# A lag of two steps and a larger share of expert work in an attention and expert kernel

## The chip, the cores and the metric

The kernel runs on one core of one Trainium2 chip. The metric is the device time of one execution in microseconds (us). A core has five engines that run side by side and wait for each other through semaphores: TensorE (PE, matrix products; PEld is its loading of the stationary operand), VectorE (DVE), ScalarE (ACT), GpSimd (POOL) and SyncE (SP), which in this kernel issues nearly all transfers (DMA).

## The reference, cut to what matters

Three stages follow each other on the same 2304 rows of 512 numbers: an attention whose mask lets each block of 64 positions see its own and all earlier blocks, four experts that all rows go through, and a last pair of products with a softmax-like gate and a normalisation.

```python
# q, k, v: (4 sequences, 8 heads, 576 positions, 64)
scores = SCALE * q @ k.T
scores = where(block_i >= block_j, scores, -1e9)
attn = exp(scores - max);  attn = attn / (sum(attn) + 1e-9)
x = attn @ v                                   # to (2304, 512)
p = domain_probs / (sum(domain_probs) + 1e-9)
for e in range(4):                             # w1: 512 x 1024, w2: 1024 x 512
    h = maximum(x @ w1[e], 0)
    out += p[:, e:e + 1] * (h @ w2[e])
h = out @ w_in;  e = exp(h - max);  sm = e / (sum(e) + 1e-9)
ln = normalised(h * sm) * g_ln
return ln @ w_out
```

## The kernel before

**Tiles.** The rows are cut into 18 token tiles of 128 rows, numbered by `TILES` (line 35): tiles 0 and 1 hold the first blocks of two sequences each, and then each sequence has four tiles, i = 1 to 4, whose rows see 64 + 128 i keys (192, 320, 448, 576). The attention goes through 84 steps: two for tile 0 and two for tile 1, four (two heads each) for a tile with i of 1 to 3, eight (one head each) for one with i = 4. Counted from 0, tile 3 begins at step 8, tile 7 at 28, tile 13 at 56, tile 14 at 64, and tile 17 ends with step 83.

**A step.** It has three parts. `step_a` (line 568) is the scores: on PE the query in two parts times the keys (L600, L601) and a mask product (L604) into one of two PSUM places `sps`, then on DVE the maximum (L606 or L608) and its scaling (L610). `step_b` (line 614) is the softmax: ACT's exponential (L639, tile `p`) and its copy to fp16 (L643, `hl`), DVE's remainder (L644, `hl`), and one transposing DMA `pT<-hl` that SP issues (L651, shown as L86, since all of SP's transfers go through a helper). `step_c` (line 656) is the product with the values, `pv<-v,pT` on PE (L670), 64 columns a matmul. `hl` has two places, `pT` has two, and `pv` has one.

**Lag.** `step()` (line 834) emits the scores and the softmax of step n, and then the products of all steps up to n - LAG, with LAG = 1. A tile's last product is followed by `finish` (line 694): DVE divides by the sums (L706 to L712), the rows are scaled, split in two fp16 parts and transposed (`xT<-xh`).

**Expert work.** All matrix operands are split in two fp16 parts, so a product of the experts is three matmuls. A hidden chunk (`emit_h`, line 294) is 12 matmuls per 128 hidden columns and row group (L305, `hps`; 384 columns each for a group of three tiles), which ACT (L313) and DVE (L314) take out of PSUM as `hch`; an output (`emit_o`, line 318) is 24 matmuls of 512 columns (L325, `ops`), added up on DVE (L349). `hps` and `ops` share three PSUM places. The tokens go through the experts in two parts: part 1 is tiles 0 to 5, part 2 is tiles 6 to 17. While the attention runs, the kernel works on part 1 with all four experts and on part 2 with the first; the other experts on part 2 and the last two products come after it. The weights are loaded by SP into one place `stage` in four pieces, squared on ACT (L126) for a scale, and split on ACT (L260) and DVE (L263) into one of three places `wt`; the steps of this are spread over the expert units (line 968). Rows that have been through the last expert are transposed as `x2T<-xh` (line 392).

**What sets the order.** The loop at line 999 emits either an attention step or an expert unit. It keeps two running costs: `tdv` grows with each attention step by 1.2 times the DVE cost that `cost()` (line 848) gives, `tpe` by the PE cost of steps and expert units. An attention step comes when `tdv <= tpe + 2`, so an expert unit is emitted whenever DVE is estimated to be ahead:

```python
if not ok or tdv <= tpe + 2.0:
    at1.step()
    a, c = at1.cost()
    tdv, tpe = tdv + a * 1.2, tpe + c
```

The emitted program then goes through a scheduler that fixes each engine's order by its own estimates of time: what is emitted earlier has priority, but an instruction that it thinks not ready is passed by later ones. On the chip each engine takes its instructions in that fixed order. A place of a pool that is taken anew waits until the last reader of what lay there is done.

**Places of part 2.** The pool `xT1` holds the transposed rows of part 2 in four places, `xT0` to `xT3`, one for three tiles each. Until tile 6 and later need them they hold operands of the first tiles; `xT3` (tiles 15 to 17) holds two pieces of the first sequence's values (`vrs[1]`, line 872).

Of the kernel before, what the change touches and what calls it, by code (L numbers as in the profile page):

```python
# [9 lines left out]
F16 = mybir.dt.float16  # L10
# [10 lines left out]
NT, D, F, E = 2304, 512, 1024, 4  # L21
# [5 lines left out]
PBITS = 14  # L27
# [4 lines left out]
LAG = 1  # L32

# Token tiles: the first blocks of two sequences together, the other blocks by two.
TILES = [(0, 0), (2, 0)] + [(b, i) for b in range(NB) for i in range(1, 5)]
# The tokens go through the experts in two parts; groups of token tiles: (first, number).
# [10 lines left out]
def group(t):  # L47
    """The group of a token tile, and its columns there."""
    for x in range(2):
        for g, (a, n) in enumerate(GROUPS[x]):  # L50
            if a <= t < a + n:
                return (x, g), (t - a) * 128
# [3 lines left out]
def tile_kernel(  # L56
# [19 lines left out]
    class InOrder:  # L76
        """An engine that takes what is given to it while strict in the order given."""
# [44 lines left out]
    def squares(x, out, junk=None):  # L122
        """The sums of the squares along the rows of x; junk: a place for the squares."""
        if junk is None:
            junk = jp.tile([128, 1024], BF16, tag="junk", name="junk")[:, :x.shape[1]]
        return act.activation(out=junk, in_=x, func=AF.Square, accum_out=out)  # L126

    def scale_bits(T, bits, s, inv):
        """s, inv = 1 / s: powers of two with 2^(bits - 0.5) <= s * sqrt(T) < 2^(bits + 0.5)."""
# [9 lines left out]
    def after(ins, other):  # L139
        """Schedules ins behind other."""  # L140
        tc.add_manual_dep(
            ins.ins, other.ins.name, mybir.DependencyInfo(mybir.DependencyClass.NoSync, mybir.DependencyReason.DATA),
            reason="pace",
        )
# [3 lines left out]
    def bg_(ins, kind):  # L148
        """Work in the background: behind what attention has of the kind so far."""
# [10 lines left out]
    def w_steps(key, src, bits, inv, tag, load_eng, rows=None, hi_eng=None, place_raw="stage"):  # L160
        """The steps of a weight's way into SBUF; each is a function to call."""
# [17 lines left out]
        def to32(c):  # L179
            """float64, as two words, rounded to float32 (to zero below float32's normal range)."""  # L180
# [113 lines left out]
    def emit_h(e, t0, k, fs, pool):  # L294
        """Hidden chunks fs of the k token tiles from t0."""
# [22 lines left out]
    def emit_o(e, o0, pool):  # L318
        """The second product for one token tile."""
# [33 lines left out]
    def fetch():  # L353
        """The sums that had no place in SBUF while attention ran."""
# [7 lines left out]
    def coef_of(e, t):  # L362
        """p_e of a tile's tokens over the scales of its products."""
# [17 lines left out]
    def split_rows(x, bits, inv, pool, tag):  # L381
        """x scaled by rows and in two parts; inv: the scales' reciprocals."""
# [13 lines left out]
    def phase_units(j, runs, pool):  # L396
        """The units of work of expert j % E on the tokens of part j // E."""
# [32 lines left out]
    # ================= attention =================  # L430
    class Attention:
        """The attention, by steps."""

        def __init__(self, bufs):
# [26 lines left out]
            # loads run ahead of their uses by as many as there are places  # L461
# [5 lines left out]
        # -- operands --  # L467
# [7 lines left out]
        def parts(self, hi, lo, raw, ps, mode):  # L475
            """raw in two float32r parts, the second on the partitions ps only."""
# [15 lines left out]
        def k_near(self, p):  # L492
            """The keys that the first tile of the first sequence needs, of one pair of heads."""
# [73 lines left out]
        # -- one step: scores of one or two heads, their softmax, times the values --  # L567
        def step_a(self, n):
# [40 lines left out]
            # exp(x - max) 2^PBITS: the factor is the sum's too  # L609
# [4 lines left out]
        def step_b(self, n):  # L614
# [35 lines left out]
            tt = self.tp.tile([128, 18, 128], F16, tag="pT", name="pT")  # L650
# [5 lines left out]
        def step_c(self, n):  # L656
            """Returns the tile that is complete after this step, if one is."""
# [36 lines left out]
        def finish(self, t):  # L694
            """The steps from a tile's products to its rows in xT."""
# [36 lines left out]
        # -- what has to be emitted before a step --  # L732
# [25 lines left out]
        def start(self):  # L758
            """The operands of the first tiles."""
# [15 lines left out]
        def second_loads(self):  # L775
            """Of the first tile's values; of the second tile; of the third one's queries."""
# [56 lines left out]

        def step(self):
            """Emits the next step."""
# [3 lines left out]
            while self.nc < min(self.n - LAG, self.NS):  # L839
# [8 lines left out]
        def cost(self):  # L848
            """Of the step emitted last: the vector engine's time and the tensor engine's."""
# [7 lines left out]
    # ================= emission =================  # L857
# [12 lines left out]
    # what part 2 will need later holds the operands of the next tiles until then  # L870
# [30 lines left out]
    # the startup's steps; the key: what they wait for, and the steps  # L901
# [19 lines left out]
    def token(c, left=0):  # L921
        """A step of the startup, or all but so many, after the loads it needs."""
# [45 lines left out]
    def spread(units, *spans):  # L968
        """Tasks among the units: each span (from, to, tasks) spreads its tasks over a part of them."""
# [29 lines left out]
    while at1.more:  # L999
        t, u, cost = moe[-1] if moe else (-1, None, 0)  # L1000
        ok = t is None or t in ready and len(bg) <= n1
        if not ok or tdv <= tpe + 2.0:
            at1.step()
            a, c = at1.cost()
            tdv, tpe = tdv + a * 1.2, tpe + c
# [46 lines left out]
    def m2_h(t):  # L1052
# [28 lines left out]
        # r = csc / (sm + 1e-9); a = r / sqrt(var r^2 + 1e-6)  # L1081
# [8 lines left out]
        # 1 / sqrt(u): halving the exponent's bits, then Newton's steps  # L1090
# [118 lines left out]
```

## Time and profile before

| | |
|---|---|
| timed runs, median of 3 | 1146.97 us (1143.22 to 1151.44) |
| span of the profiled execution | 1143.6 us |
| busy in it: PE, PEld, DVE, ACT, POOL | 1100.8, 615.7, 711.2, 504.0, 188.6 us |
| clock granted to TensorE, mean | 0.994 |
| attention: first and last product with the values | 25.0 to 404.9 us |

How to read it: the profile is one execution. A busy time is the union of an engine's instructions; the ends of matmuls are modelled, and they overlap, so a matmul's own duration is longer than the distance to the next one. "Idle before" is the time in which an engine had nothing running, put down to what released it last. The granted clock is 1.0 at 2.4 GHz and 0.5 at 1.2 GHz.

### The profile page before, as it was taken

Reading aid. Unit: us, or ns where it says so; the run is one execution under the profiler, and the core shown is the slowest. Engines: PE = TensorE matmul, PEld = TensorE weight load, DVE = VectorE, ACT = ScalarE, POOL = GpSimd, SP = SyncE. Lnnn points to the kernel's source line nnn. Section 1 sums busy time; section 2 is a strip of 40 time slices with the busy share of each in tenths; the row PEclk is TensorE's granted clock in tenths of the full one; section 3 lists DMA queues with packets and bytes.
Section 4 is the critical chain, followed back from the end, with each engine's and each line's share of the span. In section 5 each row is a group of like instructions: output and inputs, shape, how many; then the busy total and the mean of one; then the engine's idle time right before and its main releaser. Section 6 shows DMA issues by size and latency. Waiting matters only on the chain.

```text
span 1143.6 us, 18599 instructions
## 1 busy us (share of the span) xinstructions
PE 1100.8 (96%) x7232; PEld 615.7 (54%) x7232; DVE 711.2 (62%) x1560; ACT 504.0 (44%) x1067; POOL 188.6 (16%) x176
## 2 busy tenths in 40 slices
PE   6599999999999999999999999999999999999998
PEld 4466766555656655555555555555555554444443
DVE  6898688879787775231223223232698646999883
ACT  5666678668666754341332214141334332333222
POOL 4974534733631000000000000000000000000000
PEclk9999999999999999999999999999999999999999
DMA  8876998888976653120130102020122111353333
GB/s 284 259 161 161 241 198 209 213 197 182 233 167 120 151 176 87 40 74 11 46 130 4 71 1 74 1 74 1 74 83 93 28 29 28 71 105 74 83 83 83
DMA packets 216057, 125.78 MB, mean 110 GB/s; under 512 B 183712, under 2 KB 185760, under 8 KB 215456
## 3 DMA queue, kind: packets, MB, share of 16 engines
q1 hardware_dynamic: 215968, 124.59, 42.9%
q8 instruction: 57, 0.93, 0.3%
q14 instruction: 32, 0.26, 0.1%
HBM read 73.18 MB, written 6.29 MB: 69 GB/s over the span
## 4 chain that ended last, share of the span: by engine, by line
PE 79%; DVE 7%; DMA 6%; POOL 2%; issue 2%; ACT 2%; SPq 0%; ACTq 0%; DVEq 0%; POOLq 0%
PE hps L305 29%; PE ops L325 27%; PE h L1060 8%; PE o L1123 8%; DMA pT<-hl 4%; PE pv L670 2%; PE sps L600 2%; DVE hl L644 2%; DVE wt L263 2%; DMA stage<-in_w_dram 1%; PE sps L601 1%; PE sps L604 1%; ACT p L639 1%; DMA raw<-in_kZ_dram 1%; POOL wt L256 1%
## 5 line engine op out<-in xcount | busy, mean ns | idle before, releaser
L305 PE MATMUL hps<-xT,wt 128*128 128x384 f16 (+1 forms) x2688 | 396.5, 307 | 0.9 <-DVE hch L314 0.8
L325 PE MATMUL ops<-wt,hch 128*128 128x512 f16 x1728 | 385.4, 380 | 2.7 <-DVE wt L263 1.8
L305 PEld LDWEIGHTS <-wt 128*128 128x128 f16 x2688 | 241.8, 100 | 141.2 <-issue 4.6
L325 PEld LDWEIGHTS <-hch 128*128 128x128 f16 x1728 | 166.7, 98 | 196.7 <-issue 3.7
L314 DVE SCALAR_TENSOR_TENSOR hch<-hps,hch 128x384 f16<-128x384 f32 (+1 forms) x194 | 106.3, 550 | 145.9 <-ACT hch L313 145.3
L313 ACT ACTIVATE hch<-hps 128x384 f16<-128x384 f32 (+1 forms) x194 | 93.5, 484 | 233.9 <-PE hps L305 233.6
L639 ACT ACTIVATE p<-sps,nm 128x320 f32<-128x320 f32 (+4 forms) x144 | 79.0, 552 | 76.4 <-DVE nm L610 59.6
L263 DVE SCALAR_TENSOR_TENSOR wt<-stage,ws,wt 128x1024 f16<-128x1024 f32 x72 | 98.1, 1385 | 11.1 <-ACT wt L260 10.3
L126 ACT ACTIVATE junk<-stage 128x1024 bf16<-128x1024 f32 x72 | 75.9, 1054 | 63.3 <-DMA stage<-in_w_dram 49.9
L644 DVE TENSOR_TENSOR hl<-p,hl 128x320 f16<-128x320 f32 (+4 forms) x132 | 88.0, 681 | 22.4 <-ACT hl L643 22.0
L1060 PE MATMUL h<-wt,x2T 128*128 128x512 f16 x432 | 95.5, 379 | 0.8 <-DVE acc L349 0.8
L1123 PE MATMUL o<-wt,lt 128*128 128x512 f16 x432 | 95.5, 379 | 0.0
L349 DVE SCALAR_TENSOR_TENSOR acc<-ops,coef,acc 128x512 f32<-128x512 f32 x54 | 40.3, 747 | 87.7 <-PE ops L325 87.5
L600 PE MATMUL sps<-ks,qhi 128*128 128x288 f32 (+3 forms) x160 | 64.9, 409 | 12.9 <-ACT p L639 7.9
L260 ACT ACTIVATE wt<-stage,ws 128x1024 f16<-128x1024 f32 x64 | 70.7, 1139 | 4.0 <-DVE ws L137 4.0
L1060 PEld LDWEIGHTS <-x2T 128*128 128x128 f16 x432 | 42.2, 98 | 52.0 <-issue 1.1
L1123 PEld LDWEIGHTS <-lt 128*128 128x128 f16 x432 | 42.3, 98 | 51.0
L643 ACT ACTIVATE hl<-p 128x320 f16<-128x320 f32 (+4 forms) x132 | 65.3, 521 | 9.9 <-DMA pT<-hl 9.3
L670 PE MATMUL pv<-v,pT 128*128 128x64 f16 x1392 | 53.3, 196 | 8.8 <-DMA pT<-hl 8.3
L1073 ACT ACTIVATE ex<-h,nb,cs 128x1024 f32<-128x1024 f32 x18 | 21.7, 1206 | 84.4 <-DVE nb L1070 43.6
L670 PEld LDWEIGHTS <-pT 128*128 128x128 f16 x1392 | 48.8, 100 | 17.5 <-DMA pT<-hl 11.9
L601 PE MATMUL sps<-ks,qlo 128*128 128x288 f32 (+3 forms) x160 | 50.0, 316 | 1.0 <-POOL qlo L482 1.0
(127 smaller groups left out, 953.9 us busy)
## 6 DMA issues: line engine op xcount, KB each, us to landing
stage<-in_w_dram SPq DMA_DIRECT2D x64, 512.0 KB, 5.5
raw<-in_qT_dram SPq DMA_DIRECT2D x34, 256.0 KB, 3.4
vraw<-in_vC_dram SPq DMA_DIRECT2D x30, 256.0 KB, 3.1
raw<-in_kT_dram SPq DMA_DIRECT2D x24, 288.0 KB, 3.7
raw<-in_w_in_dram SPq DMA_DIRECT2D x4, 1024.0 KB, 6.2
raw<-in_w_out_dram SPq DMA_DIRECT2D x4, 1024.0 KB, 4.9
out_dram<-o2s SPq DMA_DIRECT2D x16, 256.0 KB, 2.2
raw<-in_kT_dram SPq DMA_DIRECT2D x8, 192.0 KB, 3.9
```

What stands on the lines that cost most here:

```text
L126: return act.activation(out=junk, in_=x, func=AF.Square, accum_out=out)
L263: stage["last"] = vec.scalar_tensor_tensor(out=lo, in0=r, scalar=stage[key, "s"], in1=hi, op0=ALU.mult, op1=ALU.subtract)
L305: pe.matmul(ps[:, j * n:j * n + n], w[:, a, kk, f * 128:(f + 1) * 128], x[:, b * KD + kk, c0:c0 + n], start=(m == 0), stop=(m == 3 * KD - 1),)
L313: nc.scalar.activation(out=h[:, 0, :n], in_=ps[:, :n], func=AF.Relu)
L314: nc.vector.scalar_tensor_tensor(out=h[:, 1, :n], in0=ps[:, :n], scalar=0.0, in1=h[:, 0, :n], op0=ALU.max, op1=ALU.subtract)
L325: pe.matmul(ps, hch[f][:, a, o0:o0 + 128], w[:, b, f, :], start=(m == 0), stop=(m == 3 * KF - 1))
L600: pe.matmul(o, hi[:, h % 4], rhs, start=True, stop=False)
L639: act.activation(out=dst, in_=src, func=AF.Exp, bias=nm[:, j + x:j + x + 1], scale=SCALE, accum_out=sums[:, h:h + 1],)
L644: anc["D"] = vec.tensor_tensor(out=hl[:, W + c0:W + c0 + n_], in0=pf[:, 0:n_], in1=hl[:, c0:c0 + n_], op=ALU.subtract)
L670: pe.matmul(o, tt[:, a * nch + c, :], v[:, bb, hs], start=(m == 0), stop=(m == total - 1))
L1060: pe.matmul(ps[:, half], x[:, a * KD + kk, c:c + 128], w[:, b, kk, half * 512:half * 512 + 512], start=(m == 0), stop=(m == 3 * KD - 1),)
L1123: pe.matmul(ps, tt[:, a * KF + f], w[:, b, f], start=(m == 0), stop=(m == 3 * KF - 1))
```

## The change

Three things change; the rest of the diff removes comments and adds blank lines, by which line numbers grow by 3 to 10.

1. A new method `lag()` replaces LAG in `step()`: as long as the next product belongs to a tile from 2 to 13, the products lag the scores by two steps, else by one as before. The order of the first steps, written out by hand, keeps LAG.
2. In tiles 3 to 13, a step whose number can be divided by 3 puts its `pT` into the place `xT3` of part 2's pool in place of one of the two `pT` places.
3. The running cost `tdv` grows by 1.2 times the DVE cost only up to the 29th step; from then on it grows by 5.0 us more than `tpe` does with each step, so that about 5 us of expert work are emitted per step.

```diff
+FREE = 14
+SLOW, PACE = (30, 5.0)
...
-            tt = self.tp.tile([128, 18, 128], F16, tag="pT", name="pT")
+            if 3 <= t < FREE and n % 3 == 0:
+                tt = xps[1].tile([128, 18, 128], F16, tag="xT3", name="pT")
+            else:
+                tt = self.tp.tile([128, 18, 128], F16, tag="pT", name="pT")
...
+        def lag(self):
+
+            return 2 if 2 <= self.steps[min(self.nc, self.NS - 1)][0] < FREE else LAG
+
         def step(self):
...
             self.token_a()
             while self.nb < min(self.n, self.NS):
                 self.token_b()
-            while self.nc < min(self.n - LAG, self.NS):
+            while self.nc < min(self.n - self.lag(), self.NS):
                 self.token_c()
...
             at1.step()
             a, c = at1.cost()
-            tdv, tpe = tdv + a * 1.2, tpe + c
+            tdv, tpe = tdv + (a * 1.2 if at1.n < SLOW else PACE + c), tpe + c
```

No instruction is added or removed: PE has 14042 rows in its order before and after, POOL and SP have the same number too, and DVE and ACT only merge differently. PE's order is the same up to its row 558 and nearly the same up to about row 1000; it is the same again from about row 8340 of the changed kernel to the end.

**DVE at the beginning of tile 11 (steps 48 and 49).** The rows are the fp16 remainders of the softmax (`hl<-p`, 320 columns), the score maxima (`nm<-sps`) and their scaling, the division by the sums of the tile before (`xf<-pv`), and the hidden chunks that DVE takes out of PSUM (`hch<-hps`). Before:

```order
L610 TENSOR_SCALAR nm<-nm 128x2
L644 TENSOR_TENSOR hl<-p_3568,hl 128x320
L314 SCALAR_TENSOR_TENSOR hch<-hps,hch 128x384
L644 TENSOR_TENSOR hl<-p_3572,hl 128x320
L712 TENSOR_TENSOR xf<-pv,ri 128x512
L606 TENSOR_REDUCE nm<-sps 128x2
```

And now (line numbers are higher by 3):

```order
L317 SCALAR_TENSOR_TENSOR hch<-hps,hch 128x384
L647 TENSOR_TENSOR hl<-p_4054,hl 128x320
L317 SCALAR_TENSOR_TENSOR hch<-hps,hch 128x384
L647 TENSOR_TENSOR hl<-p_4058,hl 128x320
L551 TENSOR_REDUCE vt_4759<-vt_4295 128x1
L317 SCALAR_TENSOR_TENSOR hch<-hps,hch 128x384 x2
L609 TENSOR_REDUCE nm<-sps 128x2
```

From the first `hl` of the step to the next score maximum there was one hidden chunk, and now there are three. Over the 52 maxima from the 32nd to the 84th the hidden chunks on DVE grow from 37 to 67, the outputs added up (L349) from 12 to 18, and the weight pieces split (L263) from 20 to 32.

**SP at the beginning of tile 14 (steps 64 to 67).** The rows are the transfers in the order in which SP issues them: `pT<-hl` of tile 13 (18 blocks) and of tile 14 (6 blocks), loads of operands (`raw`, `vraw`) and of weights (`stage`), and the transposed rows of finished tiles (`xT`) and of part 1 behind its last expert (`x2T`). Before:

```order
L86 DMA_TRANSPOSE pT<-hl 128x18x128
L86 DMA vraw<-in_vC_dram 128x512
L86 DMA raw<-in_qT_dram 128x512
L86 DMA_TRANSPOSE pT<-hl 128x6x128
L86 DMA stage<-in_w_dram 128x2x512 x2
L86 DMA vraw<-in_vC_dram 128x512
L86 DMA_TRANSPOSE pT<-hl 128x6x128
```

And now:

```order
L89 DMA_TRANSPOSE pT<-hl 128x18x128
L89 DMA stage<-in_w_dram 128x2x512 x4
L89 DMA_TRANSPOSE x2T<-xh 128x8x128 x2
L89 DMA_TRANSPOSE pT<-hl 128x6x128
L89 DMA vraw<-in_vC_dram 128x512
L89 DMA raw<-in_qT_dram 128x512
L89 DMA vraw<-in_vC_dram 128x512
L89 DMA_TRANSPOSE x2T<-xh 128x8x128
L89 DMA_TRANSPOSE pT<-hl 128x6x128
```

Four pieces of a weight and two transposes of part 1 now stand ahead of tile 14's first `pT`, and a third ahead of its second. Over the whole attention from step 31 on, 8 sets of weight loads stand among the `pT` transposes where there were 5, and so do the 6 `x2T` of part 1, which stood behind the last `pT` before.

## Rows read from the trace of the kernel before

**Rows 1.** The page: span and PE; busy us, share, instructions.

```profile
span 1143.6 us, 18599 instructions
PE 1100.8 (96%) x7232; PEld 615.7 (54%) x7232; DVE 711.2 (62%) x1560; ACT 504.0 (44%) x1067; POOL 188.6 (16%) x176
```

**Rows 2.** Busy time by stretch: length, then PE, PEld, DVE, ACT, POOL; clock, DMA.

```profile
0.00:80.00 80.00, 56.07 (x450) 41.20 (x451) 66.67 (x139) 47.64 (x141) 58.09 (x61) 0.98 0.81 237
80.00:150.00 70.00, 64.97 (x777) 47.97 (x774) 54.87 (x118) 47.43 (x119) 37.63 (x33) 0.98 0.81 196
150.00:300.00 150.00, 143.42 (x1269) 89.60 (x1268) 122.59 (x251) 109.71 (x262) 66.89 (x59) 0.98 0.92 208
300.00:405.00 105.00, 103.04 (x937) 64.02 (x933) 76.50 (x162) 65.40 (x156) 26.03 (x25) 1.00 0.69 152
405.00:440.00 35.00, 34.22 (x188) 17.91 (x185) 24.91 (x48) 17.26 (x32) 0.00 (x0) 1.00 0.49 151
440.00:600.00 160.00, 160.00 (x866) 84.59 (x864) 48.04 (x96) 56.25 (x97) 0.00 (x0) 1.00 0.20 65
600.00:1143.00 543.00, 539.09 (x2767) 270.43 (x2764) 317.61 (x749) 160.29 (x260) 0.00 (x0) 1.00 0.21 56
```

**Rows 3.** PE's waits in 80 to 150 us: total, times, longest.

```profile
PE pv L670 <- DMA pT<-hl: 2.8, 2, 2.2
PE sps L600 <- issue: 1.0, 1, 1.0
```

**Rows 4.** PE's waits in 150 to 316 us.

```profile
PE pv L670 <- DMA pT<-hl: 4.2, 3, 1.6
PE sps L600 <- ACT p L639: 2.1, 2, 1.5
```

**Rows 5.** PE's waits in 316 to 440 us.

```profile
PE pv L670 <- DMA pT<-hl: 1.4, 3, 0.6
PE hps L305 <- DVE hch L314: 0.8, 1, 0.8
PE sps L600 <- ACT p L639: 0.5, 1, 0.5
```

**Rows 6.** Busy time by stretch around the low clock, columns as in rows 2.

```profile
123.00:127.00 4.00, 4.00 (x28) 3.04 (x29) 2.60 (x6) 2.31 (x5) 1.40 (x2) 0.57 1.11 286
235.00:240.00 5.00, 5.00 (x21) 2.58 (x21) 5.00 (x10) 1.31 (x4) 1.46 (x2) 0.66 0.21 36
290.00:295.00 5.00, 5.00 (x22) 2.61 (x22) 3.83 (x10) 3.57 (x9) 4.75 (x5) 0.66 1.10 270
```

**Rows 7.** PE in order of time at 288 us: start, us, instruction, idle before.

```profile
288.85 0.87 PE L670 MATMUL pv<-v,pT 128*128 128x64 f16 x24 [1.45 <-DMA pT<-hl]
...
290.50 5.10 PE L305 MATMUL hps<-xT,wt 128*128 128x384 f16 x20
```

**Rows 8.** The chain that ended last, behind the attention: start, us, what.

```profile
453.12 15.60 PE hps L305 x96
468.72 15.54 PE ops L325 x72
```

**Rows 9.** DVE in order of time: the maxima of steps 29 and 30.

```profile
152.15 1.54 DVE L606 TENSOR_REDUCE nm<-sps 128x2 f32<-128x640 f32 x2
```

**Rows 10.** The products with the values: ns min/median/max, first and last start.

```profile
L670 PE MATMUL pv<-v,pT x1392: 189/193/261, 25.0 to 404.9; 128*128 128x64 f16 x199
```

**Rows 11.** DVE by line in 150 to 440 us: count, busy us, mean ns.

```profile
L263 DVE SCALAR_TENSOR_TENSOR wt<-stage,ws,wt 128x1024 f16<-128x1024 f32 x24 | 32.6, 1361 | 3.1 <-ACT wt L260 3.0
L314 DVE SCALAR_TENSOR_TENSOR hch<-hps,hch 128x384 f16<-128x384 f32 (+1 forms) x51 | 27.8, 548 | 17.7 <-ACT hch L313 17.5
```

**Rows 12.** Waits of SP's queue in 150 to 440 us.

```profile
SPq L86 <- DVE hl L644: 49.3, 28, 7.6
SPq L86 <- PE pv L670: 16.3, 8, 4.6
SPq L86 <- DVE wt L263: 14.8, 4, 5.9
SPq L86 <- DVE xh L389: 13.1, 1, 13.1
```

## The prediction

> **What bounds the kernel now.** I read the page first: PE is busy for 1100.8 of 1143.6 us [rows 1]. Then the stretches [rows 2]: behind 440 us PE has no idle time up to 600 and 543.00 - 539.09 = 3.9 us from there on, while DVE and ACT are far from full. There the 72 matmuls of 512 columns of an output take 15.54 us, 216 ns each, and 96 of 384 columns take 15.60, 162 ns each [rows 8]: that is matmul behind matmul, and this change can win nothing there. Since no instruction is added or removed, the time can change only by PE's idle time and by its low clock, ahead of 440 us.
>
> This is what lies there. From 0 to 80 us PE is idle for 80.00 - 56.07 = 23.9 us, but PE's order is nearly unchanged that far, so this stays. From 80 to 150 us it is 70.00 - 64.97 = 5.0 us; from 150 to 440 us it is 6.58 + 1.96 + 0.78 = 9.3 us [rows 2]. The waits explain both: the product waits for its transposed softmax (`pv` for `pT`) for 2.8, 4.2 and 1.4 us in three stretches, the scores wait for ACT to empty `sps` for 2.1 and 0.5, and a hidden chunk waits once, 0.8, for DVE [rows 3 to 5]. The granted clock adds a loss that no idle time shows: in 4 us at 0.57 (4 x 0.43 = 1.72 us) and in two stretches of 5 us at 0.66 (1.70 each) a part of the work ran at 1.2 GHz [rows 6]. The fall at 290.5 us followed 1.45 us in which PE waited for `pT` [rows 7]: the 20 matmuls that take 5.10 us there would take 3.3 at the distance of rows 8. So all that can be won is 5.0 + 9.3 + 5.1 = 19.4 us, of which 9.3 + 3.4 = 12.7 lie where the new pace holds.
>
> The Trainium skill (Perfetto Trace Analysis, Identifying the Most-Contended Engine) calls the matmul busy share a bad measure and would have LDWEIGHTS' share read instead. By it 150 to 300 us, with 89.60 of 150 us [rows 2], would have some 60 us to give, and the sum would be several times mine. The trace disagrees on this kernel: from 440 to 600 us the share is lower still, 84.59 of 160, and the matmuls there stand one behind the other [rows 2, 8]. The sum goes by idle time and clock.
>
> **The change, part by part.** *Where the new pace starts and ends.* The maxima of steps 29 and 30 run at 152 us [rows 9], and the last product at 404.9 [rows 10]; the 53 steps in between take 253 us, 4.8 each. The order moves 30 hidden chunks and 6 added outputs, with outputs of the first expert that ACT writes, from behind the attention into it. At 12 x 162 ns a chunk takes 1.95 us of PE and an output 24 x 216 ns = 5.18. Counting PE's order at these distances, the last product stands some 119 us of PE work later, so a step would take about 7.0 us, and the attention would end near 525 us. That is neither a gain nor a loss: the same work is missing behind it.
>
> *What the pace relieves.* DVE is busy for 122.59 + 76.50 = 199 of 255 us [rows 2]. Into the longer attention come 30 chunks at 0.548, 12 weight pieces at 1.361 [rows 11] and 6 outputs, about 0.7 each as an estimate between the two: some 37 us, and 236 / (255 + 119) = 63% where it was 78%. The chain from scores to `pT` goes through DVE and ACT, so it gets shorter, and a score that waited for ACT has a step's worth of expert work ahead of it. I take the score waits from 2.6 to 0.6 us: **-2.0**.
>
> *Lag and third place.* One would think that a lag of two puts more work between scores and product. The order doesn't show it: the scheduler had placed the products late already. Counted at the distances of the trace, PE's work between a step's last score and its first product is on average 13.6 us before and 13.6 now in steps 8 to 23, 15.2 and 15.4 in steps 32 to 63, and 14.0 and 12.7 in steps 64 to 83. The lag alone is therefore worth next to nothing; a product's wait falls only if `pT` lands sooner. The third place helps there: SP stood 16.3 us in 8 waits for a product to free a `pT` place [rows 12]. Of the 2.8 us ahead of 150 I save 0.5 (order and load are about the same there), of the 4.2 in 150 to 316, 2.8, and of the 1.4 behind, where neither lag nor third place holds, 0.5: **-3.8**. Bounds: nothing, and all 8.4.
>
> *Clock.* The two falls behind 150 us cost 1.7 each [rows 6]. One goes with the waits: **-1.7**; bounds 0 and -3.4, or -5.1 with the one at 123 us.
>
> *What it costs.* More expert work between the softmax work asks DVE and ACT for PSUM places more often. 51 chunks made PE wait for 0.8 us once [rows 5, 11]; 30 more at that rate would cost 0.5, and at 0.8 each 24 us. I take **+0.5**, the lower end, since `hps` and `ops` come up for reuse in the new order after a median of 6 us of PE work, and the rate was measured in a denser DVE. The Trainium skill (TensorE: Matmul & The Clock Gate, Architectural detail) has ACT and DVE as strict first-in, first-out queues: a chunk must wait for softmax work that stands ahead of it. The single wait of 0.8 us agrees that it can reach PE; the rule has no price. SP's queue gets 3 more sets of weights and 6 transposes of part 1 among the `pT`: below nothing there is no reason to go, and above the price is that of the third rival. I take **+0.5**. `xT3` costs nothing: DVE has read both pieces of values there long before step 9 in either order. Tile 13's last product and tile 14's first, where the lag falls from two to one, stand 5 us of PE work apart or more in the new order, and finishing a tile takes three short DVE instructions.
>
> **The sum.** -2.0 - 3.8 - 1.7 + 0.5 + 0.5 = -6.5 us: 1143.6 - 6.5 = 1137.1 us. The median of the runs is 3.4 us above the profiled span (1146.97 and 1143.6), so I forecast 1140.5 us, said as **1140**. A measurement of this kernel tells about 1% from no change, 11.5 us: 1135.5 to 1158.4 counts as the same.
>
> **The rivals.** *More than that.* With DVE at 63%, nearly every wait behind 150 us goes, both falls of the clock with them, and half of the early ones: 8.3 + 3.4 + 2.5 + 0.9 = 15 us, so 1132. For it speaks that all waits of rows 4 and 5 stand in stretches where DVE or the DMA engines (0.92 and 0.69 busy) are full; against it that the scheduler puts a product exactly where it thinks `pT` lands, so an error of its estimate shows whatever the load. Chance 0.25.
>
> *The change doesn't do what it says.* The lag adds no work ahead of the products (the counts above), and the pace only moves the end of the attention; the waits stay and move with the steps. Only the score waits shrink: -2, so 1145. Chance 0.25.
>
> *SP's queue ends it on the other side.* It issues in order, so a weight load that waits for its place `stage` (14.8 us in 4 waits, longest 5.9), or an `x2T` that waits for its rows (13.1 us, once), holds up every `pT` behind it [rows 12]. 9 such items are new among the `pT`. At 3.7 us each (14.8 / 4), and all of it passed on to PE, that is 33 us: 1140 + 33 = 1173. It decides from 0.7 us per item (6.5 / 9), and counts as slower from 2.0 us per item (18 / 9). For it speaks the order at tile 14, where four pieces and two `x2T` stand ahead of the first `pT`, and the lag there is one again; against it that a `pT` that is late by 3 us still lies within 13 us of PE work. I take 2.0 to 3.7, 1158 to 1173. Chance 0.10.
>
> **The numbers.** The forecast has 0.40, for 1136 to 1143; the rivals 0.25, 0.25 and 0.10. Faster by over 1% is the first rival, 0.25; slower is the third, 0.10; the same is 0.65. The range leaves out the lowest part of the first rival (all 19.4 us would be 1127.6) and the third: 1131 to 1150. The price of 0.8 us per chunk (+24) lies outside too.
>
> **What would show it.** Right: PE idle behind 150 us and up to the attention's end at about 5 us or less in place of 9.3, `pv` waiting for `pT` less than 3 us there, scores waiting for ACT about 0.6 or less, one fall of the clock, and the last product with the values at about 525 us; idle time ahead of 80 us and behind 600 as before. Wrong: `pv` waits as long as before (second rival); SP's waits for `wt` and `xh` grow and new `pv` waits stand at tiles 14 to 17 (third); PE waits for `hch` by more than 2 us in all (the PSUM places). A last product that comes at about 405 us again would make the whole account wrong.

## The result, and the profile after

The changed kernel takes 1151.43 us (median of 18 runs, 1149.92 to 1158.0) against 1146.2 for the kernel before (18 runs on the same chip). The ratio is 1.0052, 95% interval 1.0038 to 1.0065: half a per cent slower, by the bound of 1% the same. The forecast was 1140 with a range of 1131 to 1150, so time and range were both missed, and on the slow side.

The line numbers grow by 3 to 6: `hps` is L308, `ops` L328, the scores L603, the products with the values L676, the exponential L642, SP's helper L89. The page of the changed kernel, as [rows 1]:

```profile
span 1150.9 us, 18571 instructions
PE 1099.2 (96%) x7232; PEld 616.4 (54%) x7232; DVE 711.3 (62%) x1560; ACT 504.3 (44%) x1067; POOL 183.4 (16%) x176
```

PE's busy time fell by 1.6 us, so the span's 7.3 more are 8.9 us of idle time more (51.7 against 42.8), less 1.6. Busy time by stretch of the changed kernel, columns as in [rows 2]; the last two rows are its stretches of low clock behind 150 us, as [rows 6]:

```profile
0.00:80.00 80.00, 53.09 (x427) 38.58 (x428) 67.04 (x139) 47.12 (x140) 57.95 (x61) 1.00 0.79 234
80.00:150.00 70.00, 63.23 (x769) 47.07 (x767) 54.94 (x106) 46.16 (x116) 34.38 (x31) 0.98 0.88 194
150.00:200.00 50.00, 46.38 (x465) 31.34 (x462) 36.81 (x82) 32.49 (x81) 14.37 (x12) 0.93 0.68 154
200.00:220.00 20.00, 14.85 (x81) 8.77 (x80) 13.09 (x32) 15.62 (x31) 10.92 (x10) 0.74 1.08 241
220.00:300.00 80.00, 78.82 (x589) 46.32 (x588) 48.55 (x99) 43.84 (x105) 19.93 (x19) 1.00 0.58 155
300.00:405.00 105.00, 102.44 (x786) 60.06 (x785) 70.24 (x142) 63.65 (x138) 34.35 (x32) 1.00 0.69 162
405.00:440.00 35.00, 34.85 (x254) 19.95 (x252) 26.44 (x61) 19.74 (x51) 6.37 (x8) 1.00 0.51 98
440.00:530.00 90.00, 89.17 (x674) 52.39 (x673) 47.66 (x104) 51.56 (x110) 5.16 (x5) 1.00 0.46 113
...
158.00:166.00 8.00, 5.71 (x52) 4.81 (x53) 5.02 (x13) 5.41 (x17) 1.88 (x2) 0.57 0.87 234
206.00:217.00 11.00, 8.37 (x47) 5.55 (x48) 8.73 (x26) 9.84 (x23) 8.63 (x8) 0.53 0.94 227
```

Behind 150 us the loss is in two places. In the 20 us from 200 PE is busy for 14.85, at a clock of 0.74; and from 158 to 166 us it is busy for 5.71 of 8, at 0.57, with waits of 2.03 us for `pT` and 1.56 for `xT`, to which part 4 of the experiments comes back. Behind 220 us the change does better than the kernel before: 1.18 us idle up to 300 us at a clock of 1.00, where it was 2.99 at 0.96. The first 80 us have 3.0 us more idle than before, but a kernel below has 27.0 us there too and is the fastest of all, so that isn't the cause; the kernel before had 4 us at a clock of 0.57 there (from 65 us), and the changed one has none. PE's waits in 80 to 150, in 150 to 316 and in 316 to 530 us, as [rows 3 to 5]:

```profile
PE pv L676 <- DVE xh L730: 2.3, 1, 2.3
PE sps L603 <- POOL qlo L485: 1.9, 1, 1.9
PE pv L676 <- DMA pT<-hl: 1.8, 3, 1.0
...
PE sps L603 <- ACT p L642: 3.7, 2, 2.1
PE pv L676 <- DMA pT<-hl: 3.5, 2, 2.0
PE hps L308 <- DMA xT<-xh: 1.6, 1, 1.6
PE hps L308 <- DVE hch L317: 1.2, 1, 1.2
...
PE pv L676 <- DMA pT<-hl: 3.5, 5, 1.0
```

Scores that wait for ACT should have fallen from 2.6 to 0.6 us; they stand at 3.7, both near 205 us. There ACT, PE and SP of the changed kernel read, in order of time:

```profile
202.59 1.06 ACT L129 ACTIVATE junk<-stage 128x1024 bf16<-128x1024 f32 x1 [2.40 <-DMA stage<-in_w_dram]
203.55 0.19 ACT L129 ACTIVATION_READ_ACCUMULATOR junk<-stage 128x1 f32 x1
203.64 0.72 ACT L642 ACTIVATE p<-sps,nm 128x576 f32<-128x576 f32 x1
```

```profile
200.74 1.63 PE L308 MATMUL hps<-xT,wt 128*128 128x384 f16 x9
204.51 0.40 PE L603 MATMUL sps<-ks,qhi 128*128 128x288 f32 x1 [2.15 <-ACT p L642]
...
207.20 0.61 PE L603 MATMUL sps<-ks,qhi 128*128 128x288 f32 x1 [1.57 <-ACT p L642]
...
210.13 1.46 PE L676 MATMUL pv<-v,pT 128*128 128x64 f16 x24 [1.44 <-DMA pT<-hl]
```

```profile
198.61 1.85 SPq L89 DMA_DIRECT2D stage<-in_w_dram  x4
200.57 5.47 SPq L89 DMA_TRANSPOSE pT<-hl  x1
```

`junk<-stage` squares a quarter of a set of weights to find its scale. It stands in ACT's queue ahead of an exponential of tile 9, and its load left SP only at 198.61 us, so ACT waits 2.40 us, the exponential with it, and the scores with the exponential. A second square does the same at 205.28 us, behind a wait of 0.82. The same four loads are ahead of the transposition of `pT`, and the chain that ended last runs through it there, not through the square:

```profile
198.61 1.96 DMA stage<-in_w_dram
200.57 9.51 DMA pT<-hl
```

This `pT` landed 9.51 us after SP took it up, where the median in this kernel is 3.9. So both hold PE here: the square (2.15 and 1.57 us) and the `pT` behind the loads (1.44). This is the fifth set of weights: the pace had moved it out of tile 8 into tile 9 (steps 36 to 43); before, its loads left SP from 175.95 us on.

### The profile page after: what moved, and what is told of

The parts are those of the page before. It is cut to its first block, busy times and chain, and to the rows that moved or that the text cites. A ratio compares the mean times of both kernels' runs of the same rounds, so it can differ in the third digit from the quotient of the medians.

```text
span 1150.9 us, 18571 instructions
## 1 busy us (share of the span) xinstructions
PE 1099.2 (96%) x7232; PEld 616.4 (54%) x7232; DVE 711.3 (62%) x1560; ACT 504.3 (44%) x1067; POOL 183.4 (16%) x176
## 3 DMA queue, kind: packets, MB, share of 16 engines
q1 hardware_dynamic: 215968, 124.59, 42.8%
## 4 chain that ended last, share of the span: by engine, by line
PE 80%; DMA 8%; DVE 6%; POOL 2%; issue 2%; ACT 1%; SPq 0%; ACTq 0%; POOLq 0%; DVEq 0%
PE ops L328 30%; PE hps L308 28%; PE h L1070 8%; PE o L1133 8%; DMA pT<-hl 5%; PE pv L676 2%; PE sps L603 2%; DVE wt L266 2%; DVE hl L647 1%; PE sps L604 1%; DMA vraw<-in_vC_dram 1%; PE sps L607 1%; DMA stage<-in_w_dram 1%; POOL wt L259 1%; DVE nm L609 1%
## 5 line engine op out<-in xcount | busy, mean ns | idle before, releaser
L308 PE MATMUL hps<-xT,wt 128*128 128x384 f16 (+1 forms) x2688 | 396.6, 306 | 2.7 <-DMA xT<-xh 1.6
L328 PE MATMUL ops<-wt,hch 128*128 128x512 f16 x1728 | 385.6, 380 | 4.4 <-DVE wt L266 3.7
L308 PEld LDWEIGHTS <-wt 128*128 128x128 f16 x2688 | 239.8, 100 | 137.5 <-issue 3.5
L328 PEld LDWEIGHTS <-hch 128*128 128x128 f16 x1728 | 167.2, 98 | 198.4 <-issue 7.5
L642 ACT ACTIVATE p<-sps,nm 128x320 f32<-128x320 f32 (+4 forms) x144 | 78.9, 552 | 84.8 <-DVE nm L613 55.5
L603 PE MATMUL sps<-ks,qhi 128*128 128x288 f32 (+3 forms) x160 | 68.1, 429 | 16.2 <-ACT p L642 9.0
L263 ACT ACTIVATE wt<-stage,ws 128x1024 f16<-128x1024 f32 x64 | 70.4, 1141 | 4.3 <-DVE ws L140 4.3
L676 PE MATMUL pv<-v,pT 128*128 128x64 f16 x1392 | 55.1, 196 | 11.3 <-DMA pT<-hl 8.8
L676 PEld LDWEIGHTS <-pT 128*128 128x128 f16 x1392 | 49.0, 100 | 20.7 <-DMA pT<-hl 14.4
```

Source lines behind the costliest of these rows:

```text
L308: pe.matmul(ps[:, j * n:j * n + n], w[:, a, kk, f * 128:(f + 1) * 128], x[:, b * KD + kk, c0:c0 + n], start=(m == 0), stop=(m == 3 * KD - 1),)
L328: pe.matmul(ps, hch[f][:, a, o0:o0 + 128], w[:, b, f, :], start=(m == 0), stop=(m == 3 * KF - 1))
L603: pe.matmul(o, hi[:, h % 4], rhs, start=True, stop=False)
L642: act.activation(out=dst, in_=src, func=AF.Exp, bias=nm[:, j + x:j + x + 1], scale=SCALE, accum_out=sums[:, h:h + 1],)
L676: pe.matmul(o, tt[:, a * nch + c, :], v[:, bb, hs], start=(m == 0), stop=(m == total - 1))
```

## The experiments

All ratios are against the kernel before on the same chip, with a 95% interval.

**1. The parts alone.** Each undoes parts of the change:

```diff
# no pace
-            tdv, tpe = tdv + (a * 1.2 if at1.n < SLOW else PACE + c), tpe + c
+            tdv, tpe = tdv + a * 1.2, tpe + c
# no third place
-            if 3 <= t < FREE and n % 3 == 0:
+            if False:
# no lag
-            return 2 if 2 <= self.steps[min(self.nc, self.NS - 1)][0] < FREE else LAG
+            return LAG
```

Lag and third place: 

> Lag of two and third pT place as in the change; the pace is that of before. Theory P (the third place lets the scheduler put four value loads ahead of the pT of tile 7 near 150 us, the product waits, the clock falls): +3 to +5 us against before, with PE waits for pT and xT near 158 us and a low clock behind them as in the changed kernel. Theory W (weight loads and their squares on ACT, brought into the attention by the pace, stand ahead of the softmax): within 1.5 us of before, because the weights stand where they stood. The forecast's account (third place saves waits): -2 to -4 us.

Pace: 

> The pace of the change alone; lag 1 and two pT places. Theory P: within 1.5 us of before or faster by the 2 to 4 us that I forecast for the pace (score waits and clock). Theory W: +3 to +6 us, with ACT waiting for a weight load, scores waiting for ACT near 200 us and a low clock behind them.

Lag: 

> The lag of two alone; two pT places and the old pace. The orders of SP and POOL are those of before, and PE's differs in 50 of 14042 rows. Both theories: within 1 us of before. If it is off by 3 us or more, the lag acts in a way that the order doesn't show.

Third place: 

> The third pT place alone; lag 1 and the old pace. SP's order up to 160 us is that of the lag with the third place. Theory P: +3 to +5 us, like the lag with the third place. Theory W: within 1.5 us of before.

| parts | ratio | interval |
|---|---|---|
| lag | 1.0010 | 0.9993 to 1.0027 |
| third place | 1.0039 | 1.0025 to 1.0053 |
| pace | 1.0025 | 1.0011 to 1.0039 |
| lag, third place | 1.0076 | 1.0056 to 1.0097 |
| all three | 1.0052 | 1.0038 to 1.0065 |

The lag is worth nothing by itself; the third place costs, with or without it, and so does the pace: each theory had a part of the loss. Lag and third place together cost some 9 us, more than the 3 to 5 expected; why they cost more than the place alone stays open. The pace alone has the loss of the changed kernel in the same 20 us, with more score waits (5.2 us at 205.2 and 1.4 ahead of it). Busy time from 200 to 220 us of the kernel before, of the pace alone, and of the run of part 2 with pace and earlier loads:

```profile
200.00:220.00 20.00, 19.37 (x149) 11.16 (x149) 18.51 (x29) 11.30 (x20) 15.00 (x12) 1.00 0.70 193
```

```profile
200.00:220.00 20.00, 13.20 (x74) 8.10 (x74) 12.84 (x32) 16.37 (x31) 11.64 (x11) 0.66 0.98 242
```

```profile
200.00:220.00 20.00, 20.00 (x129) 10.76 (x127) 12.15 (x25) 11.37 (x21) 6.54 (x7) 1.00 0.72 210
```

**2. The weights of step 32 loaded earlier.** To the pace alone and to the whole change; and the third place from tile 7 on only, with lag and old pace, and in the whole change with earlier loads.

```diff
-    bg += [(14, fn) for fn in p2 + q2] + [(32, fn) for fn in p3]
+    bg += [(14, fn) for fn in p2 + q2] + [(28, fn) for fn in p3[:5]] + [(32, fn) for fn in p3[5:]]
# third place from tile 7
-            if 3 <= t < FREE and n % 3 == 0:
+            if 7 <= t < FREE and n % 3 == 0:
```

Pace, earlier loads: 

> The pace alone (no lag, no third place), and the five steps that load the weights emitted after attention step 32 are emitted from step 28; the squares of those weights stay at step 32. The program's order: the four loads stand between the 29th and the 30th transposition of pT instead of the 32nd and the 33rd, and the scheduler sets the four squares among the 448-wide steps of tile 8 instead of the 576-wide steps of tile 9. Theory W (a square in ScalarE's queue waits for a load that is issued too late, the exponentials behind it wait with it, and the clock falls after that): the waits of scores for ACT at 198 to 212 us (1.41, 5.2 and 0.85 us in the pace alone) shrink to under 1 us together, the 13.7 us of low clock behind them go or shrink to 3.4, and the time goes from ratio 1.0025 to about 0.993 to 0.997 (1138 to 1143 us). Rival R (the tensor engine lacks expert work there, since the pace spent it earlier, whatever the loads do): the waits stay over 4 us, ratio 1.002 to 1.004.

All, earlier loads: 

> The whole change, with the same earlier loads as in the run before. Theory W: the waits of scores for ACT at 204 to 208 us (2.15 and 1.57 us) and for pT at 210 (1.44) fall by about 4 us together, and the 10.2 us of low clock behind them by 7 to 10, half of which is lost: 1143 to 1147 us, ratio 0.997 to 1.001. What the third place costs at 115 to 161 us (idle 80 to 150 us 6.8 against 5.0 before, and about 5 us from 150 to 165) stays. Rival R: 1150 to 1152 us, ratio 1.004 to 1.006.

Lag, third place from tile 7: 

> The lag and the third place with the old pace, the third place used from tile 7 on instead of tile 3. SP's order is then that of the kernel before up to the 38th transposition. Theory P (the third place costs because from tile 3 on it lets the scheduler bring the loads of the values and of the weights in front of pT and xT near 150 us): idle from 80 to 220 us goes back to 8 to 9 us (before 8.6, lag and place from tile 3 11.7), no low clock near 147 and 164 us, ratio 0.998 to 1.003 against 1.0076. Rival Q (the place costs wherever it is used, by transfers that meet or by waits after 220 us, where lag and place had 9.3 us of idle time against 5.7): ratio 1.004 to 1.008.

All, earlier loads, third place from tile 7: 

> The whole change with both mends: weights of step 32 loaded from step 28, third place from tile 7. W and P both right: idle 80 to 220 us about 9 us (before 8.6, after 15.6), idle 220 to 440 us about 3 to 4 (before 5.7, after 3.9), low clock 3 to 7 us in all: 1136 to 1141 us, ratio 0.991 to 0.996. W alone right: as the run e8_early, 0.997 to 1.001. P alone right: the waits for ACT near 205 us stay, 1146 to 1149 us, ratio 1.000 to 1.003. Neither: 1.005.

Measured: 0.9943 (0.9921 to 0.9965), 0.9956 (0.9943 to 0.9970), 1.0048 (1.0030 to 1.0066) and 0.9924 (0.9905 to 0.9943). The first and the last are what theory W, and W and P together, gave; the second is better than W gave, and the third lies in the range of rival Q. The 200 to 220 us are full in all three with the earlier loads. One thing in the expectation was described wrongly: the loads that moved from the 32nd to the 29th transposition are those of the fifth weights, the next ones. The edit has the fourth weights' scale written two steps sooner; the scheduler then places their splits earlier (ACT does the last of them at 174.40 us, in the pace alone at 190.25), so the place `stage` comes free and the fifth weights' loads leave at 178.28 us in place of 196.44.

Putting the place off to tile 7 gave back 0.3 points in either setting. Without the pace, lag and place were still 0.5% slower than the kernel before, 0.4 points more than the lag alone, so theory P doesn't hold the whole cost; PE's waits for `pT` behind 150 us were 6.8 us there, in 7 places, and what makes them stays open.

**3. Is it the loads?** Earlier loads in the kernel before; pace, lag and earlier loads without the place; the pace alone with the fifth weights' squares freed from their loads; and no lag, with the place from tile 7.

```diff
# pace alone; i == 4: the fifth weights
+                if inv is not own[0]:
...
+                after(act.activation(
+                    out=junk.rearrange("p (a c) -> p a c", a=8), in_=ones.unsqueeze(1).to_broadcast([128, 8, 128]),
+                    func=AF.Square, scale=0.02, accum_out=stage[key, "t"][:, c:c + 1],
+                ), anc["A"])
...
+        if i == 4:
+            own[0] = inv
```

Before, earlier loads: 

> The kernel before (old pace, lag 1, no third place) with the one edit of the last runs: the five loading steps of the weights of step 32 emitted from step 28. A control: is what that edit gave under the pace (ratio 1.0025 to 0.9943) a gain that the kernel before would have had as well? In the kernel before the scores wait 0.6 us at 217 and nothing between 190 and 217 us, so if the edit only undoes what the pace did wrong (theory W), it gives nothing here: ratio 0.998 to 1.002 (it moves other loads too: two of the next weights' loads go one transposition later). If earlier loads are a gain by themselves (rival G): 0.992 to 0.995.

Lag, pace, earlier loads: 

> Pace, lag and earlier loads, without the third place: with the run e7 (0.9943, without lag and place) and the run e10 (0.9924, place from tile 7) it parts the lag from the place. The prediction gave lag and place 3.8 us of shorter waits for pT together. The last run with all of them has waits for pT of 0.99, 1.65, 0.70, 0.65, 0.63 and 1.04 us from 150 us on, 5.7 us, the run e7 0.84, 1.26, 1.14 and 2.72, 6.0 us. If the lag alone carries what there is: ratio 0.991 to 0.994. If it does as little as it did by itself (1.001): 0.993 to 0.996.

Pace, squares of a constant: 

> The pace alone, and the squares of the fifth weights (the first of the two groups of loads that the pace puts near 200 us) read a constant that is in SBUF instead of the place that the loads fill. The sums of squares are then not these weights' own, and their scale is that of the constant; nothing else is left out. The squares keep their number, their length and their place among the exponentials of tile 9, and the four loads stay between the 32nd and the 33rd transposition, ahead of pT. Theory W, narrow (the square's wait for its load holds the exponentials behind it): the waits of scores for ACT near 199 to 212 us (7.5 us) fall under 2 us, the low clock behind 202 us goes, ratio 0.994 to 0.998. Rival S (the four loads in SP's queue delay the transposition of pT that stands behind them, and ACT's square is only beside it): pT of that step lands as late, the waits stay over 4 us, ratio 1.001 to 1.004. Rival T (the 4.9 us of squares and 4.6 us of splits stand on ACT between the exponentials of tile 9, whether they wait or not): scores wait for ACT 3 to 5 us, ratio 0.998 to 1.001.

Pace, earlier loads, third place from tile 7: 

> Pace, earlier loads and the third place from tile 7, without the lag. With lag 1 a transposition has one step to land, so a place that comes free earlier only helps if places were short: if the place carries the difference between 0.9943 and 0.9924, ratio 0.991 to 0.993; if lag and place only help together, or neither does, 0.994 to 0.996.

Measured: 1.0086 (1.0062 to 1.0110), 0.9923 (0.9898 to 0.9948), 1.0001 (0.9982 to 1.0020) and 0.9952 (0.9933 to 0.9971). With the earlier loads the lag is worth 0.2 to 0.3 points (0.9943 to 0.9923 without the place, 0.9952 to 0.9924 with it), though the intervals overlap, and the place from tile 7 nothing.

Freed squares: no score waits for ACT between 150 and 220 us any more, as the narrow theory said, but half of the time came back as another wait of PE, and the ratio is the one that rival T gave (not by its mechanism):

```profile
204.84 0.59 PE L255 MATMUL tp<-wt,ones 128*128 128x1 f32 x2 [4.18 <-DVE wt L253]
```

`tp` sums the squares of the fifth weights over the partitions. It stands in PE's queue right behind the scores of tile 9, and waits there from 200.66 us; the last square ends at 203.0, and DVE comes to their reduction at 204.64. So it isn't one square's wait alone: freeing it gave back 0.2 of the 0.8 points that the earlier loads give (intervals that overlap), and another step of the weights' chain then stood in an in-order queue too early for when it could run. On rival S this run tells little: in the pace alone `pT` left SP only at 204.28 us, 5.8 us behind the loads, and landed in 4.5, while in the changed kernel it followed them at once. Squares freed in the whole change were not run. The kernel before with earlier loads shows the chain on a third engine. DVE and PE, in order of time:

```profile
204.93 0.16 DVE L243 TENSOR_REDUCE wt<-wt 128x1 f32<-128x4 f32 x1 [7.14 <-ACT junk L126]
```

```profile
210.18 5.08 PE L325 MATMUL ops<-wt,hch 128*128 128x512 f16 x15 [3.70 <-DVE hch L314]
```

DVE's queue waits 7.14 us for the last square, with the remainders and hidden chunks of others behind it, and PE 3.70 for one of those. So the edit is no gain by itself; it moves the chain, and where the chain falls decides. That the same edit costs 0.9% here I had not expected: from 200 to 220 us PE is busy for 15.29 us where it was 19.37, which makes 4.1 of the 10 us, and more by a clock of 0.91; the rest lies elsewhere and isn't followed here.

A held queue needn't cost: with pace and earlier loads ACT waits three times as long as in the changed kernel, at 212.89, with an exponential right behind it, and PE is never idle there, since it has expert outputs in its queue. ACT and PE of that run:

```profile
212.89 1.06 ACT L129 ACTIVATE junk<-stage 128x1024 bf16<-128x1024 f32 x1 [7.46 <-DMA stage<-in_w_dram]
213.85 0.19 ACT L129 ACTIVATION_READ_ACCUMULATOR junk<-stage 128x1 f32 x1
213.94 0.72 ACT L642 ACTIVATE p<-sps,nm 128x576 f32<-128x576 f32 x1
```

```profile
211.16 5.13 PE L328 MATMUL ops<-wt,hch 128*128 128x512 f16 x23
```

In the changed kernel PE's queue had 9 chunk matmuls, 1.63 us, ahead of the waiting scores, and the next outputs stood behind them, at 213.67 us.

**4. Two that were left open.**

Lag and pace: 

> Lag and pace without the third place, and without the earlier loading steps: the run e12 (0.9923) less that one edit, and the whole change less the place. The fifth weights' four loads stand between the 32nd and the 33rd transposition again. Theory W' (those weights' whole chain - loads, squares, the product of one column that sums them - falls among the exponentials of tile 9 when it starts at 196 us, and beside long expert work when it starts at 178): the tensor engine is idle 5 to 10 us from 195 to 215 us with low clock of 6 to 14 us behind it, ratio 1.000 to 1.004. Rival L (that the edit of the loading steps gave anything was a chance arrangement; with the lag the pace alone is good): 0.992 to 0.996, and idle under 3 us there.

```diff
# all, earlier loads
+            if "xT" in marks and t == 6:
+                after(x, marks["xT"])
...
+                marks["xT"] = sync.dma_start_transpose(out=xtile(xT, t, "xT"), in_=xh.rearrange("p a f -> p (a f)"))
```

All, earlier loads, `xT` ahead: 

> The whole change with the earlier loading steps (e8: 0.9956, idle 4.3 us from 150 to 220 us, of it 2.5 us for xT at 159.5, and 6.8 us of low clock from 159) and one order more: the transpositions of pT of tile 6 may not go ahead of the transposition of xT that was written before them. In SP's order xT of tile 5 then stands after the 22nd transposition of pT; in e8 it is after the 24th, with five loads of values ahead of it, in the kernel before after the 23rd. The third place still begins at tile 3. Theory P (the place costs near 155 us because xT goes behind one more transposition and the value loads): the wait for xT goes, at most 1 us of other waits comes in its place, the low clock at 159 us goes, ratio 0.991 to 0.994 as with the place from tile 7. Rival P2 (the transposition of pT that now stands behind xT is late instead): pv waits 1.5 to 3 us near 150 to 158 us, ratio 0.995 to 0.997.

Lag and pace: 1.0007 (0.9985 to 1.0029); from 200 to 220 us PE is busy for 13.38 at a clock of 0.74. With the earlier loads that pair has 0.9923, so, as theory W' had it, the gain of the earlier loads is no chance arrangement of the pace alone. In those 20 us PE waits 2.76 us for ACT and, for a `pT` that landed 9.87 us after SP took it up behind the four loads, 2.90. `xT` ahead: 0.9953 (0.9936 to 0.9970), no gain over 0.9956 and the ratio of rival P2, though the new waits lie earlier than it said; the wait for `xT` fell from 2.50 to 1.46 us, and 1.01 and 0.75 us of waits for `pT` and ACT with a fall of the clock came at 144 to 147 us. The place's cost in tiles 3 to 6 thus moves when one wait is taken away.

Where the cost lies without that order shows in the run with everything and earlier loads. PE in order of time; the stretch behind it in that run, and the same stretch with the place from tile 7:

```profile
156.45 0.52 PE L676 MATMUL pv<-v,pT 128*128 128x64 f16 x12 [1.76 <-DMA pT<-hl]
159.48 1.01 PE L308 MATMUL hps<-xT,wt 128*128 128x128 f16 x8 [2.50 <-DMA xT<-xh]
```

```profile
158.00:166.00 8.00, 6.52 (x59) 5.73 (x59) 3.64 (x11) 5.47 (x18) 1.88 (x2) 0.58 0.81 218
```

```profile
158.00:166.00 8.00, 8.00 (x124) 6.84 (x122) 3.99 (x16) 6.63 (x22) 2.19 (x2) 1.00 0.97 223
```

With the place from tile 3 SP issues two more loads of values (four from 147.89 us, taking 4.80, and one at 155.21, where there are three with the place from tile 7) and one more `pT` ahead of the `xT` that the first chunks of the tile need; two waits follow, and the mean clock of the 8 us is 0.58. That this order is the cause is not shown, since the run with `xT` ahead gained nothing.

**The best version** is lag, pace and earlier loads without the third place: 1136.54 us against 1145.7, ratio 0.9923 (the one with the place from tile 7, 0.9924, can't be told from it). Its waits of PE in 80 to 150 (first row), 150 to 316 and 316 to 530 us, its products with the values, and its busy time from 150 to 530:

```profile
PE pv L676 <- DMA pT<-hl: 3.0, 2, 2.3
...
PE pv L676 <- DMA pT<-hl: 0.6, 1, 0.6
PE hps L308 <- DMA xT<-xh: 0.2, 1, 0.2
...
PE pv L676 <- DMA pT<-hl: 1.6, 3, 1.1
```

```profile
150.00:530.00 380.00, 377.46 (x2953) 224.53 (x2953) 250.79 (x531) 228.71 (x516) 88.31 (x84) 1.00 0.63 153
```

## Why the prediction was wrong, step by step

The terms of the sum, with what the changed kernel and the best version measured (us; before from [rows 3 to 6]):

| term | before | forecast | changed | lag, pace, earlier loads |
|---|---|---|---|---|
| scores wait for ACT, behind 150 us | 2.6 | 0.6 | 3.7 | 0 |
| `pv` waits for `pT`, behind 150 us | 5.6 | 2.3 | 7.0 | 2.2 |
| the same, 80 to 150 us | 2.8 | 2.3 | 1.8 | 3.0 |
| `hps` waits for `hch`, `xT`, behind 150 us | 0.8 | 1.3 | 2.8 | 0.2 |
| stretches of low clock behind 150 us | 2 | 1 | 2, longer | 0 |

**The attention's end**, forecast at about 525 us: right; the last product starts at 532.4 us (404.9 before).

```profile
L676 PE MATMUL pv<-v,pT x1392: 192/193/242, 25.2 to 532.4; 128*128 128x64 f16 x199
```

DVE's share, forecast at 63%, came out right too: 36.81 + 13.09 + 48.55 + 70.24 + 26.44 + 47.66 = 242.8 of 380 us, 64%.

**What the pace relieves**, the term of -2.0: in the best version no score waits behind 150 us, as forecast and more (that a less dense DVE is the reason is argued, not shown); in this kernel the score waits grew. The step that failed is that I read the pace as an even stretch. At its start it also changes which step each set of weights falls beside. I costed the weights behind tile 14, where sets were added, and not the fifth set, which was moved from tile 8 to tile 9. What that place is worth is the difference that the earlier loads make: with pace 0.8 points (1.0025 to 0.9943), in the whole change 1.0 (1.0052 to 0.9956), 9 to 11 us, for which the sum had no term.

**SP's queue**, taken at +0.5, with a rival at 1158 to 1173 for weight loads ahead of `pT`. The mechanism was the right one to fear, but it came at another place, and on ACT too: behind 400 us, at tiles 14 to 17, PE waited for `pT` for 0.15 and 0.83 us only (SP's four waits for `wt` are 12.3 us, 14.8 in [rows 12], and the one for `x2T`'s rows 1.9, 13.1 there), while four loads in front of a `pT` at 198.61 us held that `pT` until 210.08 and, through the square, the exponentials on ACT. That a queue keeps its order is what the traces show on ACT, PE and DVE in turn; I had priced it only for hidden chunks and, at 0.5 us, for SP. (The rule that the prediction cites from the Trainium skill, TensorE: Matmul & The Clock Gate, Architectural detail, agrees: 2.40 us on ACT and 7.14 us on DVE.)

**Lag and third place**, -3.8. That the lag adds no work ahead of the products was right (1.0010). That the third place would help was the other wrong step: 3.3 us for it and the pace behind 150 us were read from SP's 16.3 us of waits for a product [rows 12], and 4.6 of these lie behind SP's last `pT` (398.5 us). With the old pace the place hardly changed them (14.4 us alone; 15.7 with the lag, 17.2 for the lag without it). In the changed kernel they did fall:

```profile
SPq L89 <- PE pv L676: 3.1, 5, 1.6
```

PE's waits for `pT` behind 150 us did not fall with them, 7.0 us for 5.6. Where they came to 2.2 us, beside the forecast 2.3, there was no third place at all, and SP waited 12.2 us for a product. The place from tile 3 costs 0.3 to 0.7% in four pairs (1.0039 alone, 1.0076 against 1.0010, 1.0052 against 1.0007, 0.9956 against 0.9923). I had costed the place as a buffer, and the order shows that it moved loads of keys and values and `xT` from the 15th transposition on. Ahead of 150 us, 2.3 us for `xh` and 1.9 for `qlo` are new, which the sum had not; one of them, or both, stands in all five runs with the place from tile 3 (2.3 to 2.5 and 1.9 us) and in no other.

**Clock**: forecast one stretch less behind 150 us. There are two as before, elsewhere and longer: 8 us at 0.57 and 11 at 0.53, where [rows 6] has 5 us at 0.66 twice.

**PSUM places**, +0.5: `hch` 1.2 us in one wait, nearer the lower end, as taken.

Against the list of what would show it: the end was as forecast for right; idle time behind 150 us up to the attention's end (3.62 + 5.15 + 1.18 + 2.56 + 0.15 + 0.83 = 13.5 us against 9.3), score waits and clock as for wrong. The sum itself, -6.5 us, is close to what lag and pace do once the fifth weights are out of the way: 1145.7 to 1136.5, -9.2. That is partly luck: there the waits for `pT` fell without the third place, and both stretches of low clock went where one was forecast.

## What to carry to other kernels

When a table or a pace moves the emission of anything, follow every chain of background work that moves with it - load, squares, sum, scale, split - to where it newly stands in each in-order queue, not just what was added. A wait in such a queue costs what the tensor engine lacks at that moment: look at how much work stands in PE's queue ahead of the instruction that is held up. And a third buffer is also an edit of the order; if no wait of the bound engine is put down to the lack of a place, it may only reshuffle the queue of transfers.

## What the runs showed of the hardware

- The chain of 2 MB of weights held ACT (a square that waited 2.40 us for its load), PE's own queue (a sum, 4.18 us, in the run with the squares freed) or DVE (a reduction, 7.14 us, in the kernel before with earlier loads); taking it off one engine put it on another.
- A `pT` that SP took up right behind four loads of 512 KB landed after 9.51 us (changed kernel), 9.87 (lag and pace) and 8.1 (pace and earlier loads, where PE did not wait for it); the median is 3.9 in the changed kernel.
- The same kind of hold on ACT, 7.46 us, cost nothing while PE had 23 output matmuls (5.13 us) in its queue.
- The low clock beside PE's waits: one wait of 1.45 us that ends at 288.85 us, and 5 us at 0.66 from 290 [rows 6, 7]; waits of 2.03 and 1.56 us that end at 158.73 and 161.11, and 8 us at 0.57 from 158; waits of 2.15, 1.57 and 1.44 us that end at 204.51, 207.20 and 210.13, and 11 us at 0.53 from 206.
- Why PE's busy time fell by 1.6 us in the changed kernel, although its stretches of low clock behind 150 us are longer, no run here settles.
